# Forgetting attention and a SiLU MLP on one core: v of the first blocks on the GpSimd queue, and the first scores before the weights' transposes

## The chip, the core and the metric

The kernel runs on one core of a Trainium2 chip, in one launch. The metric is the device time of one execution in microseconds (us). A core has a matrix engine (TensorE, in the profile PE for its matmuls and PEld for its weight loads), VectorE (DVE), ScalarE (ACT), GpSimd (POOL) and SyncE (SP). They run side by side, each in the order of its own program, and wait for one another by semaphores. Sixteen DMA engines move data between the chip's memory and the core. In this kernel DMAs are issued from SyncE (the profile's queue q1), from GpSimd (q0) and, at the very end, from ScalarE.

## What is computed

The reference is an attention with a decay from forget gates f, followed by a two-layer MLP over all heads side by side:

```python
scores = scale * np.matmul(q, k.transpose(0, 1, 3, 2))
log_f = np.log(np.clip(f, 0.0001, 1.0))
cum = np.cumsum(log_f, axis=-1)
decay = cum[:, :, :, None] - cum[:, :, None, :]
causal = np.triu(np.ones((S, S), dtype=bool), k=1)
scores = np.where(causal, -1000000000.0, scores + decay)
...
x = attn_out.transpose(0, 2, 1, 3).reshape(B * S, H * D)
h = x @ w_in
g = h * (1.0 / (1.0 + np.exp(-h)))
return g @ w_out
```

There are B = 8 batches of H = 8 heads, S = 576 positions and D = 64 columns a head; w_in is 512 x 2048 and w_out 2048 x 512. All inputs and the output are float32.

## The kernel before

The decay splits into a factor of the query, which cancels in the softmax, and one of the key, so the kernel multiplies v (and a column of ones beside it, which yields the softmax's denominator) by a weight per key. The weights of all batches are made once at the start: a logarithm of f, a running sum, an exp into `wexp`, five transposes on TensorE and a copy into `w_bf` (`weights_scan()` and `weights()`).

The order on each engine is written out by hand: what the program says first on an engine runs first there.

The first 128 positions of each batch are treated apart, as "first blocks", because their queries see only their own block. For each batch b: `load_qk0(b)` brings q and k in as bf16 by two DMAs on the GpSimd queue (128 rows of 2 KB each). `load_v0(b)` brings v in as float32 by one DMA on the SyncE queue (256 KB in pieces of 64 floats) into one of four buffers `vfs[b % 4]`. `turn0(b, i)` turns q (i = 0) or k (i = 1) by matmuls with a selection matrix; ScalarE or VectorE copies the result to SBUF. `ban0` writes the causal mask into a score tile by a matmul, `scores0` adds the scores to it and takes their exp, `convert_v0(b)` multiplies v by the weights on GpSimd into `v0[b]`, `out0(b)` multiplies with v and divides, `back0(b)` transposes the result into the MLP's input. Batches 0 to 3 make the MLP's first group of 512 rows (g = 0), batches 4 and 5, and 6 and 7, groups 1 and 2 of 256 rows.

The MLP's weights come in quarters on the GpSimd queue as bf16: `load_w_in(i)` brings the columns for chunks 4i to 4i + 3 of the first product, `load_w_out(i)` the rows for part i of the second. `m1_chunk` is a chunk of the first product (TensorE into `hp`, L552; a tanh on ScalarE, L560; the product on VectorE, L561). `m2_part` is one quarter of the sum for one output tile of 128 rows (L597); parts 0 to 3 of a tile follow one another, and part i reads quarter i of w_out. `fill(us)` puts MLP matmuls for about that many microseconds at its place in the program, chosen by the writer of the order from those whose inputs are ready in program order; it does not look at the run. After groups 0 and 1 are under way, `fill(6.0, 2)` is the first with second-product parts.

Then the rest of each batch (positions 128 to 575) is done in pairs of heads: `load_qk(n)`, `load_tails(b)` and `load_v(b, c)` on SyncE's queue, `cast_qk` on GpSimd, a transposing DMA on SyncE's queue (`transposes`, L421), `scores` (L453), `attend` (L498, L507), `back` (L528). The loop over these pairs takes MLP work between its steps until the end.

`after(ap)` is a tiny DMA on SyncE's queue that reads from a tile; as it waits for the tile's load, so does all that stands behind it on SyncE's queue. Before the change there are three: behind k of batch 0 (ahead of v of batches 2 and 3), behind quarter 2 of w_in (ahead of v of batches 6 and 7), and behind quarter 1 of w_out (ahead of the loads for the main attention).

The GpSimd program before reads, in order: q,k of batches 0 to 3 among small constants; fills of the ones columns; conversion of v 0, w_in quarter 0, conversions 1 and 2, w_in 1, conversion 3, q,k of 4, w_in 2, q,k of 5, w_in 3; constants; conversion 4, w_out 0 and 1, conversion 5, w_out 2 and 3, q,k of 6 and 7; conversions 6 and 7; then the casts for the main attention.

Of the kernel before, what the change touches and what calls it, by code (L numbers as in the profile page):

```python
# [12 lines left out]
P = 128  # L13
# [5 lines left out]
def kernel(  # L19
# [10 lines left out]
    nc = tc.nc  # L30

    B, H, S, D = q.shape
    DM, DFF = moe_w_in.shape
    BH = B * H
    NCC = DM // P
# [35 lines left out]
    w_in_bf = const.tile([P, NCC, DFF], BF16, name="w_in_bf")  # L71
# [49 lines left out]
    def load_qk0(b):  # L121
        t = conv.tile([P, 2, RUN * D], BF16, name="qkb", tag="qkb")
        for i, src in enumerate((q, k)):
            nc.gpsimd.dma_start(
                out=t[:, i, :],
                in_=src[b, :, 0:P, :].rearrange("h (r c) d -> r h (c d)", c=RUN),
            )
        qk0[b] = t

    def load_v0(b):  # L130
        t = vfs[b % 4]
        nc.sync.dma_start(out=t[:, :, 0:D], in_=v[b, :, 0:P, :].rearrange("h p d -> p h d"))
        vf0[b] = t

    qst: dict[int, tuple] = {}
# [42 lines left out]
    WQ = 4  # L178

    def load_w_in(i):  # L180
        c0, c1 = i * DFF // WQ, (i + 1) * DFF // WQ
        nc.gpsimd.dma_start(out=w_in_bf[:, :, c0:c1], in_=w_in_v[:, :, c0:c1])

    def load_w_out(i):
        c0, c1 = i * NFC // WQ, (i + 1) * NFC // WQ
        nc.gpsimd.dma_start(
            out=w_out_bf[:, c0:c1, :],
            in_=moe_w_out[c0 * P : c1 * P, :].rearrange("(fc p) m -> p fc m", p=P),
        )

    def after(ap):
        nc.sync.dma_start(out=junk[0:1, 0:16], in_=ap)
# [5 lines left out]
    nc.sync.dma_start(out=f_sb[:, :], in_=f.rearrange("b h s -> (b h) s"))  # L198
    load_qk0(0)
    load_v0(0)  # L200
    load_v0(1)
    after(qk0[0][0:1, 1, 0:16])
    load_v0(2)
    load_v0(3)
    make_identity(nc, ident_bf)
    load_qk0(1)
    make_identity(nc, ident_f)
# [2 lines left out]
    load_qk0(3)  # L210
    for t in vfs:
        nc.gpsimd.memset(t[:, :, D : D + 1], 1.0)
    for i in range(2):
        for g in range(2):
            nc.vector.tensor_copy(
                out=sel[:, i, :].rearrange("p (u w r) -> p u w r", u=2, w=2)[:, g, :, :],
                in_=ident_bf[:, :].rearrange("p (r u i w) -> p u i w r", u=2, i=2, w=2)[
                    :, g, i, :, :
                ],
            )  # L220

    def keep_warm(n):
# [7 lines left out]
        out=f_sb[:, :], in0=f_sb[:, :], scalar1=1e-4, scalar2=1.0, op0=ALU.max, op1=ALU.min  # L230
# [29 lines left out]
    def weights():  # L260
        wps = pbig.tile([P, NM + 1, BH], FP32, name="wps", tag="big")
        for c in range(NM + 1):
            nc.tensor.transpose(wps[:, c, :], wexp[:, c * P : (c + 1) * P], ident_f[:, :])
        nc.vector.tensor_copy(out=w_bf[:, :, :], in_=wps[:, :, :])
# [6 lines left out]
    def turn0(b, i):  # L271
        src = qk0[b]
        if i == 0:
            qT0[b] = qktp.tile([P, NP, P], BF16, name="qkT", tag="qkT")
        dst, evac = ((qT0[b], nc.scalar.copy), (kT0[b], nc.vector.tensor_copy))[i]
        tp = pbig.tile([P, NP, NRUN, RUN], FP32, name="tp", tag="big")
        for c in range(RUN):
            for j in range(2):
                nc.tensor.matmul(  # L279
                    tp[j * D : (j + 1) * D, :, :, c].rearrange("p a r -> p (a r)"),  # L280
                    lhsT=src[:, i, c * D : (c + 1) * D],
                    rhs=sel[:, j, :],
                    start=True,
                    stop=True,
                )
        evac(
            out=dst[:, :, :].rearrange("p a t -> p (a t)"),
            in_=tp[:, :, :, :].rearrange("p a r c -> p (a r c)"),
        )

    def ban0(b):
        sc = psc.tile([P, 2, NP, P], FP32, name="sc", tag="sc")
        for i in range(2):
            nc.tensor.matmul(
                sc[:, i, :, :].rearrange("p a t -> p (a t)"),
                lhsT=ident_bf[:, :],
                rhs=ban[:, :, :].rearrange("p a t -> p (a t)"),
                start=True,
                stop=False,
            )  # L300
        return sc

    def scores0(b, sc=None):
        t = qT0.pop(b)
        fresh = sc is None
        u = upool.tile([P, 2, NP, P], BF16, name="u", tag="u")
        u0[b] = u
        if fresh:
            sc = psc.tile([P, 2, NP, P], FP32, name="sc", tag="sc")
        for p in range(NP):  # L310
            for i in range(2):
                r = slice(i * D, (i + 1) * D)
                nc.tensor.matmul(
                    sc[:, i, p, :],
                    lhsT=kT0[b][r, p, :],
                    rhs=t[r, p, :],
                    start=fresh,
                    stop=fresh or p == NP - 1,
                )
        nc.scalar.activation(  # L320
            out=u[:, :, :, :].rearrange("p i a t -> p (i a t)"),
            in_=sc[:, :, :, :].rearrange("p i a t -> p (i a t)"),
            func=ACT.Exp,
            scale=scale,
        )
# [7 lines left out]
    def convert_v0(b):  # L333
        nc.gpsimd.tensor_tensor(
            out=v0[b][:, :, :],
            in0=vf0.pop(b)[:, :, :],
            in1=w_bf[:, 0, b * H : (b + 1) * H, None].to_broadcast([P, H, D + 1]),
            op=ALU.mult,
        )
# [36 lines left out]
    def back0(b, *copies):  # L376
        xq = xqs.pop(b)[:, :, :].rearrange("p (c j) d -> p c (j d)", j=2)
        g, c0 = HEADS_OF[b]
        k = NCC // len(copies)
        for n, copy in enumerate(copies):  # L380
            tx = pbig.tile([P, k, P], BF16, name="tx", tag="big")
            for cc in range(k):
                nc.tensor.transpose(tx[:, cc, :], xq[:, n * k + cc, :], ident_bf[:, :])
            copy(out=xg(g)[:, n * k : (n + 1) * k, c0 : c0 + P], in_=tx[:, :, :])
# [239 lines left out]
    def step():  # L624

        a, c = at["m1"], at["m2"]
        can1 = a < len(M1) and M1[a][0] in ready
        g1 = M1[a][0] if a < len(M1) else NG
        g2 = M2[c][0] if c < len(M2) else NG
        if can1 and M1[a][1] == 0 and g1 > g2 + 1:  # L630
            can1 = False
        can2 = open2["w"] and c < len(M2) and g2 < g1
        if not can1 and not can2:
            return None
        if can1 and can2:
            f1 = M1[a][1] / NFC
            f2 = (c - sum(M2_OF[:g2])) / M2_OF[g2]
            want = 3 - at["last"] if abs(f1 - f2) < 0.15 else (1 if f1 < f2 else 2)
            if want == at["last"] and at["row"] >= 2 and abs(f1 - f2) < 0.25:
                want = 3 - want  # L640
            can1 = want == 1
        kind = 1 if can1 else 2
        at["row"] = at["row"] + 1 if kind == at["last"] else 1
        at["last"] = kind
        if can1:
            m1_chunk(*M1[a])
            at["m1"] += 1
            return 4 * (GW[g1] / 2.4 + 2.5)
        m2_part(*M2[c])
        at["m2"] += 1  # L650
        return 4 * (DM / 2.4 + 2.5)
# [6 lines left out]
    def fill(us_, first=0, least=0):  # L658
        if first:
            at["last"], at["row"] = 3 - first, 2  # L660
        at["left"] += us_ * 1000
        while at["left"] > 0 or least > 0:
            t = step()
            if t is None:
                at["left"] = 0.0
                return False
            at["left"] -= t
            least -= 1
        return True
# [6 lines left out]
    keep_warm(1)  # L676
    turn0(0, 1)
    bans = [ban0(0), ban0(1)]
    weights()
    setup_pool.__exit__(None, None, None)  # L680
    gpool = ctx.enter_context(tc.tile_pool(name="gpool", bufs=2))
    convert_v0(0)
    load_w_in(0)
    turn0(1, 0)
    scores0(0, bans[0])
    turn0(1, 1)
    turn0(2, 0)
    turn0(2, 1)
    scores0(1, bans[1])
    convert_v0(1)  # L690
    load_v0(4)
    out0(0, apart=True)
    scores0(2, ban0(2))
    convert_v0(2)
    load_w_in(1)
    load_v0(5)
    turn0(3, 0)
    turn0(3, 1)
    bans = ban0(3)
    out0(1, apart=True)  # L700
    scores0(3, bans)
    convert_v0(3)
    load_qk0(4)
    load_w_in(2)
    load_qk0(5)
    load_w_in(3)
    back0(0, on_act)
    out0(2)
# [11 lines left out]
    convert_v0(4)  # L720
    load_w_out(0)
    load_w_out(1)
    after(w_in_bf[0:1, NCC - 1, 3 * DFF // WQ - 16 : 3 * DFF // WQ])
    load_v0(6)
    load_v0(7)
    convert_v0(5)
    load_w_out(2)
    load_w_out(3)
    load_qk0(6)
    load_qk0(7)  # L730
    after(w_out_bf[0:1, 2 * NFC // WQ - 1, DM - 16 : DM])
    load_qk(0)
    load_tails(0)
# [42 lines left out]
    fill(6.0, 2)  # L776
    two_more(6, False)
    ready.add(2)
    fill(2.5)

# [29 lines left out]
    for m in range(NQ):  # L812
# [6 lines left out]
        if m > 0:  # L819
            back(m - 1)  # L820
            if m % 2 == 0:
                b = m // 2 - 1
# [49 lines left out]
```

## Time and profile before

| | |
|---|---|
| median of 9 runs | 351.95 us (351.21 to 352.46) |
| the profiled execution, its own time | 351.41 us |
| its span, first to last instruction | 349.6 us |
| TensorE matmuls busy | 340.9 us, 98% |
| ScalarE busy | 217.4 us, 62% |
| VectorE busy | 186.9 us, 53% |
| GpSimd busy | 123.6 us, 35% |
| moved by DMA | 47.92 MB, mean 137 GB/s |
| of it on SyncE's queue | 31.75 MB in 127184 packets |
| of it on GpSimd's queue | 15.47 MB in 9376 packets |

The profile is one execution; times in it count from its first instruction. A line of a timeline gives start, length, engine, source line, operation, and the tiles written and read; in brackets stands how long the engine was idle ahead of it, and what ended that. "Busy" of TensorE takes in matmuls that wait for nothing but their own pipeline. For a DMA the engine's line is the issue alone; its landing is told apart, as the time from issue to landing.

### The profile page before, as it was taken

The page shows a single profiled execution, that of the slowest core. Times are in us where ns is not written, and L with a number is a line of the kernel's source. Part 1 is how long each engine was busy: PE and PEld are TensorE (multiplying, and loading weights), DVE is VectorE, ACT ScalarE, POOL GpSimd, SP SyncE. Part 2 cuts the span into 40 slices and gives each one's busy share as a digit, 9 for nine tenths or more (in the row PEclk, how much of TensorE's full clock was granted, in tenths as well). Part 3 has the DMA queues.
Part 4 walks back from the last instruction along what each step waited for, and adds up shares of the span by engine and source line. Part 5 has one row for each costly group of instructions (what it writes and reads, how often), then busy time and mean ns, then how long its engine had stood idle before and what let it go on. Part 6 is the DMA issues. An engine that isn't in the chain of part 4 may idle for free.

```text
span 349.6 us, 9033 instructions
## 1 busy us (share of the span) xinstructions
PE 340.9 (98%) x3644; PEld 204.8 (59%) x3644; DVE 186.9 (53%) x411; ACT 217.4 (62%) x401; POOL 123.6 (35%) x221
## 2 busy tenths in 40 slices
PE   8989999999999999999999999999999999999994
PEld 3645565576656656566565666656656565555663
DVE  4755735355676565575555564656745553534330
ACT  5856636876587675857759567595775934544431
POOL 7894145537273163083054225326320000010001
PEclk9999999999999999999999999999999999999998
DMA  8999999999897887697487688479611000010012
GB/s 154 218 207 201 196 192 176 230 190 195 187 217 170 166 149 167 144 185 162 113 188 145 145 187 149 106 169 186 130 53 35 32 32 30 30 63 30 32 60 60
DMA packets 136761, 47.92 MB, mean 137 GB/s; under 512 B 128016, under 2 KB 134416, under 8 KB 136720
## 3 DMA queue, kind: packets, MB, share of 16 engines
q1 hardware_dynamic: 127184, 31.75, 49.1%
q0 software_dynamic: 9376, 15.47, 18.6%
q8 instruction: 28, 0.46, 0.6%
q10 hardware_dynamic: 160, 0.13, 0.1%
q14 instruction: 13, 0.11, 0.1%
HBM read 36.85 MB, written 9.44 MB: 132 GB/s over the span
## 4 chain that ended last, share of the span: by engine, by line
PE 85%; DMA 7%; ACT 3%; issue 1%; POOL 1%; DVE 1%; SPq 0%; POOLq 0%; ACTq 0%
PE po L597 35%; PE hp L552 32%; PE sc L453 7%; PE dn L498 5%; PE dn L507 3%; DMA qkb<-in_q_dram 2%; PE tx L528 2%; DMA vf<-in_v_dram 2%; DMA qkT<-qkb 1%; DMA qkb<-in_k_dram 1%; ACT u L457 1%; PE tp L279 1%; ACT osb L607 1%; DVE gt L561 1%; ACT ut L469 0%
## 5 line engine op out<-in xcount | busy, mean ns | idle before, releaser
L561 DVE SCALAR_TENSOR_TENSOR gt<-th,hp 128x384 bf16<-128x384 bf16 (+2 forms) x208 | 105.3, 522 | 81.4 <-ACT th L560 78.4
L560 ACT ACTIVATE th<-hp 128x384 bf16<-128x384 f32 (+2 forms) x208 | 95.3, 479 | 85.1 <-PE hp L552 83.4
L597 PE MATMUL po<-w_out_bf,gt 128*128 128x512 bf16 (+1 forms) x592 | 146.0, 374 | 0.0
L552 PE MATMUL hp<-x,w_in_bf 128*128 128x384 bf16 (+2 forms) x704 | 130.2, 322 | 1.1 <-DVE gt L561 0.8
L552 PEld LDWEIGHTS <-w_in_bf 128*128 128x128 bf16 x832 | 78.3, 98 | 55.6 <-issue 1.4
L457 ACT ACTIVATE u<-sc 128x1024 bf16<-128x1024 f32 (+1 forms) x96 | 74.8, 818 | 16.9 <-PE sc L453 16.8
L597 PEld LDWEIGHTS <-gt 128*128 128x128 bf16 x592 | 54.9, 98 | 48.9 <-issue 2.5
L576 POOL DMA_DIRECT2D out_dram<-osb x38 | 21.0, 553 | 167.7 <-ACT osb L607 134.7
L407 POOL TENSOR_TENSOR vp<-vf,w_bf 128x520 bf16<-128x520 f32 (+1 forms) x32 | 35.5, 1112 | 15.5 <-DMA vf<-in_v_dram 14.5
L462 DVE TENSOR_TENSOR u<-u,tri 128x768 bf16<-128x768 bf16 x32 | 21.1, 660 | 24.7 <-ACT u L457 24.7
L607 ACT ACTIVATE osb<-po 128x512 f32<-128x512 f32 (+1 forms) x37 | 22.0, 594 | 13.4 <-PE po L597 13.4
L453 PE MATMUL sc<-qkT 64*128 64x128 bf16 (+1 forms) x640 | 26.3, 207 | 0.6 <-DMA qkT<-qkb 0.5
L476 DVE TENSOR_TENSOR ut<-ut,trit 128x128 bf16<-128x128 bf16 x32 | 8.8, 276 | 28.0 <-ACT ut L469 27.9
L453 PEld LDWEIGHTS <-qkT 64*128 64x128 bf16 x640 | 18.2, 94 | 9.5 <-issue 6.1
L469 ACT ACTIVATE ut<-sc 128x640 bf16<-128x640 f32 x32 | 23.0, 719 | 0.0
L498 PEld LDWEIGHTS <-u 128*128 128x128 bf16 x576 | 20.8, 98 | 3.4 <-issue 0.4
L498 PE MATMUL dn<-vp,u 128*128 128x65 bf16 x384 | 21.8, 194 | 0.0
L516 DVE TENSOR_TENSOR xr<-dn,rec 128x448 bf16<-128x448 f32 x32 | 20.0, 624 | 1.1
L498 PE MATMUL dn<-v,u 128*128 128x65 bf16 x192 | 19.8, 194 | 0.3 <-DVE gt L561 0.3
L393 POOL CAST qkb<-qf 128x384 bf16<-128x384 f32 x32 | 16.2, 507 | 10.7 <-DMA qf<-in_q_dram 8.0
L393 POOL CAST qkb<-kf 128x384 bf16<-128x384 f32 x32 | 17.0, 531 | 7.1 <-DMA kf<-in_k_dram 7.1
L552 PE MATMUL hp<-xt,w_in_bf 128*128 128x256 bf16 x128 | 17.7, 273 | 0.0
(67 smaller groups left out, 219.3 us busy)
## 6 DMA issues: line engine op xcount, KB each, us to landing
vf<-in_v_dram SPq DMA_DIRECT2D x32, 256.0 KB, 5.0
out_dram<-osb POOLq DMA_DIRECT2D x32, 256.0 KB, 2.7
qf<-in_q_dram SPq DMA_DIRECT2D x64, 96.0 KB, 2.9
kf<-in_k_dram SPq DMA_DIRECT2D x64, 96.0 KB, 3.1
w_in_bf<-in_moe_w_in_dram POOLq DMA_DIRECT2D x4, 512.0 KB, 8.3
w_out_bf<-in_moe_w_out_dram POOLq DMA_DIRECT2D x4, 512.0 KB, 12.2
qkb<-in_q_dram POOLq DMA_DIRECT2D x8, 128.0 KB, 6.0
qkb<-in_k_dram POOLq DMA_DIRECT2D x8, 128.0 KB, 6.0
```

What stands on the lines that cost most here:

```text
L393: nc.gpsimd.tensor_copy(out=t2[:, c0 : c0 + NR, :].rearrange("p c x -> p (c x)"), in_=t[:, :, :, :].rearrange("p c h d -> p (c h d)"),)
L407: nc.gpsimd.tensor_tensor(out=vbf[b][r, c, :, :], in0=vst[b][c][r, :, :], in1=w_bf[r, c + 1, b * H : (b + 1) * H, None].to_broadcast([n, H ...
L453: nc.tensor.matmul(sc[:, i, o : o + q1 - q0], lhsT=kt, rhs=t[r, q0:q1], start=True, stop=True)
L457: nc.scalar.activation(out=u[:, :, c * SM : c * SM + w], in_=sc[:, :, 0:w], func=ACT.Exp, scale=scale)
L462: nc.vector.tensor_tensor(out=x, in0=x, in1=tri[:, None, None, :].to_broadcast([P, 2, NR, P]), op=ALU.mult,)
L469: nc.scalar.activation(out=ut[:, :, 0:3:2, :].rearrange("p k i t -> p i k t"), in_=sc[:, :, T0 : T0 + (NM + 1) * ST].rearrange("p i (k t) ...
L498: nc.tensor.matmul(dn[:, i * NR + c - 1, :], lhsT=u[:, i, o : o + P], rhs=vals(kb, i), start=(kb == 0), stop=(kb == c),)
L552: nc.tensor.matmul(hp[:, :], lhsT=w_in_bf[:, cc, fc * P : (fc + 1) * P], rhs=xg(g)[:, cc, :], start=(cc == 0), stop=(cc == NCC - 1),)
L560: nc.scalar.activation(out=th[:, :], in_=hp[:, :], func=ACT.Tanh, scale=0.5)
L561: nc.vector.scalar_tensor_tensor(out=gt[:, fc, :], in0=th[:, :], scalar=1.0, in1=hp[:, :], op0=ALU.add, op1=ALU.mult,)
L597: nc.tensor.matmul(po[:, :], lhsT=gt[:, fc, tb * P : (tb + 1) * P], rhs=w_out_bf[:, fc, m0:m1], start=(fc == 0), stop=(fc == NFC - 1),)
L607: nc.scalar.activation(out=osb[:, :], in_=po[:, :], func=ACT.Copy, scale=0.5)
```

## The change

Six v loads (batches 2 to 7) move from SyncE's queue to GpSimd's. Their places in the GpSimd program: 2 and 3 behind q,k of batch 3 and the ones columns, ahead of the first conversion; 4 and 5 each behind the q,k pair of its batch; 6 and 7 likewise. The q,k pairs of 6 and 7 move ahead of w_out quarters 2 and 3, and conversion 5 ahead of them. Two of the three `after` waits go; the one behind quarter 1 of w_out stays. Apart from that, the first scores are put ahead of the weights' transposes, and one `fill(2.5)`, the last one ahead of the main attention, becomes `fill(1.0)`.

```diff
     def load_v0(b):
         t = vfs[b % 4]
-        nc.sync.dma_start(out=t[:, :, 0:D], in_=v[b, :, 0:P, :].rearrange("h p d -> p h d"))
+        q_ = nc.sync if b < 2 else nc.gpsimd
+        q_.dma_start(out=t[:, :, 0:D], in_=v[b, :, 0:P, :].rearrange("h p d -> p h d"))
...
     load_v0(1)
-    after(qk0[0][0:1, 1, 0:16])
-    load_v0(2)
-    load_v0(3)
...
         nc.gpsimd.memset(t[:, :, D : D + 1], 1.0)
+    load_v0(2)
+    load_v0(3)
...
     bans = [ban0(0), ban0(1)]
+    scores0(0, bans[0])
     weights()
...
     turn0(1, 0)
-    scores0(0, bans[0])
     turn0(1, 1)
...
     convert_v0(1)
-    load_v0(4)
...
     load_w_in(1)
-    load_v0(5)
...
     load_qk0(4)
+    load_v0(4)
     load_w_in(2)
     load_qk0(5)
+    load_v0(5)
     load_w_in(3)
...
     load_w_out(1)
-    after(w_in_bf[0:1, NCC - 1, 3 * DFF // WQ - 16 : 3 * DFF // WQ])
+    convert_v0(5)
+    load_qk0(6)
     load_v0(6)
+    load_qk0(7)
     load_v0(7)
-    convert_v0(5)
     load_w_out(2)
     load_w_out(3)
-    load_qk0(6)
-    load_qk0(7)
     after(w_out_bf[0:1, 2 * NFC // WQ - 1, DM - 16 : DM])
...
     ready.add(2)
-    fill(2.5)
+    fill(1.0)
```

## The prediction, made before the result was known

> **What bounds the kernel now.** I read four views: busy times, TensorE's stretches, the timelines of TensorE, GpSimd and SyncE up to 66 us, and the landing time of each load of that stretch. First the page and the stretches (columns: stretch, length, busy us with instructions for PE, PEld, DVE, ACT, POOL; then clock, DMA share, GB/s):
>
> ```profile
> PE 340.9 (98%) x3644; PEld 204.8 (59%) x3644; DVE 186.9 (53%) x411; ACT 217.4 (62%) x401; POOL 123.6 (35%) x221
> 5.60:17.90 12.30, 11.64 (x223) 8.14 (x223) 8.45 (x23) 9.22 (x14) 9.61 (x19) 1.00 1.26 221
> 17.90:26.20 8.30, 7.53 (x62) 3.43 (x63) 4.95 (x8) 4.38 (x8) 8.02 (x17) 1.00 1.24 206
> 41.00:61.60 20.60, 19.95 (x195) 11.39 (x193) 8.80 (x20) 9.47 (x20) 8.26 (x11) 1.00 1.15 186
> ```
>
> TensorE is full. Its idle time is 349.6 - 340.9 = 8.7 us, of which 1.2 lie before its first matmul and 9.60 - 5.22 = 4.4 after 340 us. No edit removes TensorE work, so only the small gaps between can be won: 0.66, 0.77 and 0.65 us in these three stretches. The DMA engines move some 200 GB/s without a pause in the first 46 us, so the order of the loads decides. TensorE's timeline (start, length) shows what waits for them:
>
> ```profile
> 22.04 1.90 PE L552 MATMUL hp<-x,w_in_bf 128*128 128x512 bf16 x8 [0.51 <-DVE gt L561]
> 26.17 1.27 PE L279 MATMUL tp<-sel,qkb 128*64 128x64 bf16 x32 [0.24 <-DMA qkb<-in_q_dram]
> 41.15 2.75 PE L597 MATMUL po<-w_out_bf,gt 128*128 128x512 bf16 x12
> 43.73 0.60 PE L552 MATMUL hp<-x,w_in_bf 128*128 128x256 bf16 x4
> 44.17 1.89 PE L597 MATMUL po<-w_out_bf,gt 128*128 128x512 bf16 x8
> 61.63 0.40 PE L453 MATMUL sc<-qkT 64*128 64x128 bf16 x8 [0.52 <-DMA qkT<-qkb]
> ```
>
> The gap at 22.04 is put down to DVE, but the fifth chunk of the first MoE product is the first to read quarter 1 of w_in, and that was issued at 14.00 and took 8.0 us: 22.0. So it is a DMA wait. The 12 matmuls at 41.15 are parts 0, 1 and 2 of one output tile and read quarters 0, 1, 2 of w_out; the line at 44.17 begins with part 3 and quarter 3. GpSimd's and SyncE's timelines:
>
> ```profile
> 13.00 1.05 POOL L334 TENSOR_TENSOR v<-vf,w_bf 128x520 bf16<-128x520 f32 x1 [0.56 <-DMA vf<-in_v_dram]
> 14.00 0.81 POOL L182 DMA_DIRECT2D w_in_bf<-in_moe_w_in_dram  x1
> 23.58 1.56 POOL L186 DMA_DIRECT2D w_out_bf<-in_moe_w_out_dram  x2
> 26.15 1.54 POOL L186 DMA_DIRECT2D w_out_bf<-in_moe_w_out_dram  x2
> 29.54 0.52 POOL L124 DMA_DIRECT2D qkb<-in_k_dram  x1 [0.28 <-DMA w_in_bf<-in_moe_w_in_dram]
> 26.10 1.16 SPq L132 DMA_DIRECT2D vf<-in_v_dram  x2
> 35.79 0.50 SPq L192 DMA_DIRECT2D junk<-w_out_bf  x1
> 36.34 1.11 SPq L150 DMA_DIRECT2D qf<-in_q_dram  x2
> ```
>
> Adding each issue's time to landing gives, for GpSimd's queue: w_in 17.6, 22.0; q,k of batch 4 at 22.2 and 22.9; w_in 25.4; q,k of 5 at 26.1 and 26.7; w_in 29.2; w_out 32.4, 35.8, 39.1, 42.5; q,k of 6 at 43.4 and 44.0, of 7 at 44.8 and 46.1. They land in the order of issue. SyncE's v: batches 2 to 7 at 12.85, 13.85, 18.3, 19.3, 37.8, 44.4. So w_out quarter 2 has 42.88 - 39.1 = 3.8 us in hand, quarter 3 has 44.17 - 42.5 = 1.7.
>
> [...] The trace agrees that queues share: with SyncE quiet a w_in quarter takes 2.5 us (22.9 to 25.4, 26.7 to 29.2), beside SyncE's loads a w_out quarter takes 3.2 to 3.4. [...] no v on that queue is in this trace. [...] Here the row from 17.9 to 26.2 us, nearly all large runs, shows 206 GB/s, and the same view from 61.6 to 75 us, mostly 256 B runs, 209; I see no such loss.
>
> **The change part by part.**
>
> *Issues on GpSimd.* Six v loads come in: two before the first conversion, one behind each of the q,k pairs 4 to 7. An issue there costs 0.53 us for q or k (128 runs) and 0.80 for a weight quarter (512 runs), 0.0007 us a run; v has 1024 runs: 1.16 us. Lower bound 0.55 (a store of the same 256 KB), upper 2.3 (double). The first two then occupy GpSimd from 7.5 to 9.8. The first conversion waits for w_bf anyway; the eight score matmuls now ahead of the transposes take 0.32 us (their block starts at 9.35, the next at 9.67), so w_bf moves from 9.37 to 9.7 and the conversion from 9.52 to 9.85. Cover: out0(0) needs it at 11.47 and it ends at 10.9, so 0. At 2.3 us an issue it would end near 13.2 and cost about 1.7 us. ScalarE gets its first exp about 1 us sooner and its cast of qT0(1) 0.3 later; TensorE's order after 9.7 is as before.
>
> *v of batches 2 and 3.* Now behind q,k of 1 to 3 in one queue, with the same bytes ahead (v0, v1, f and four q,k pairs: 1.72 MB). I keep 12.9 and 14.2. Conversion 2 starts at 13.0 as now, conversion 3 (14.83) stays. The removed SyncE wait for the first k costs nobody anything, as it only held these loads. Zero, from -0.3 to +1.
>
> *v of batches 4 and 5.* They leave the stretch in which w_in quarters 0 and 1 come in. 0.52 MB at 206 GB/s is 2.5 us, so quarter 1 lands near 19.5 instead of 22.0, before its chunk at 21.5: -0.51. Batch 5's q,k have only v4 of the two ahead: 1.3 us earlier, and TensorE is there 0.5 earlier: -0.23. Sum -0.74. Their conversions run at some 25.5 and 28, well before out0(4) at 32.57.
>
> *v and q,k of 6 and 7 ahead of w_out quarters 2 and 3.* This is the large one. Quarter 1 of w_out lands at 35.8 with three quarters of v6 beside it; v6 is now behind, 0.75 x 1.27 = 0.95 less, and the unmixed v may save a little: 34.6. Then, in line: q,k 6 1.3 (25.4 to 26.7), v6 1.27, q,k 7 1.3, v7 1.27, together 5.1: 39.7. SyncE's wait for quarter 1 ends at 34.6 too, so its q, k and tail loads run beside the rest: quarters 2 and 3 at 3.2 each, as now beside SyncE: 42.9 and 46.1. Bounds for quarter 3: 43.7 (v at 1.0 us as between the landings of v2 and v3, SyncE taking nothing), 47.6 ([...]1.3 more). GpSimd's issues don't limit: they run to about 35, and the eight-in-flight limit that the 29.54 line suggests (the ninth waited for the landing of the first) asks only that w_out 1 has landed for the last issue.
> TensorE's order is fixed. It wants quarter 2 at 42.88 - 0.74 = 42.1 and waits 0.8; runs part 2 (0.86) and a chunk (0.44); is at part 3 at 44.2 and waits to 46.1: 1.9. Against 44.17 before, it is 1.9 us late. Nothing makes that up later, as it is full to the end.
>
> *Attention's start.* fill(1.0) only moves about 1.5 us of MoE matmuls behind the first scores. TensorE would be there at 61.1 + 1.9 - 1.5 = 61.5. SyncE starts its loads 1.2 us sooner, so the transposed tile lands between 60.4 and 61.6: the 0.52 wait goes.
>
> Sum: 0 + 0 - 0.74 + 2.67 (the two waits) - 0.52 = +1.4 us. The profiled execution took 351.41 us, 1.8 more than its span; +1.4 gives 352.8. The median of the nine runs is 351.95, 0.54 above it: 353.3.
>
> **Rivals.**
> 1. *w_out comes in time* (ends faster). If v in line goes at 1.0 us and SyncE's loads get little, quarters 2 and 3 land at 41.2 and 43.7 and the waits are 0 and 0.3. Then -0.74 - 0.52 + 0.3, about -1.0: 350.9. For it: [...]SyncE's first loads of this stretch took 10 us to land. Against: 1.05 MB are put ahead of two quarters that had 3.8 and 1.7 us in hand. It decides when quarter 3 lands before about 44.
> 2. *Balance.* Quarter 3 at 44.6 to 45.3, so that the wait eats the gains: 351.7 to 352.4.
> 3. *v is slow on GpSimd's queue* (twice the time, 2.6 us, or 2.3 us an issue). v3 is late by some 2 us, so conversion 3, out0(3) and the start of MoE are; quarter 3 lands 6 x 1.3 = 8 us later still. About +7: 359. Against: nothing in the trace shows that queue slower by bytes.
>
> That the change doesn't do what it says is no rival: the new order is plain in the program.
>
> **How the numbers follow.** Forecast 0.46 (own range 352.5 to 355), in time 0.34, balance 0.12, slow v 0.08. A difference under 0.2%, 0.7 us, can't be told from none. Faster 0.34, same 0.12, slower 0.54. The range is from 350.6 to 355.3; it leaves out the slow v and the ends of the bounds.
>
> **What would show it.** Right: no gap near 22 and 26; TensorE idle twice between 41 and 47, ahead of po matmuls; w_out quarters 2 and 3 landing near 43 and 46, q,k of 6 before 37; no wait at the first sc of L453. Wrong: part 3 without a wait, v issues over 1.5 us on GpSimd, or a later first hp than 17.9.

## The result, and the profile after

The changed kernel takes 354.21 us (median of 10 runs, 353.72 to 356.65) where the kernel before takes 351.95 (31 runs): a ratio of 1.0071, with a 95% interval from 1.0057 to 1.0084. It is slower by 2.3 us. The forecast was 353.3 us, in a range from 350.6 to 355.3, with slower as the likeliest side.

The profiled execution took 354.75 us, its span is 353.0. That is 3.3 us above the profiled execution of before, 1 us more than the medians differ by, so the trace shows the loss a little too large.

TensorE's stretches after (same columns as before: stretch, length, busy us with instructions for PE, PEld, DVE, ACT, POOL; clock, DMA share, GB/s):

```profile
5.60:17.90 12.30, 10.78 (x220) 7.53 (x218) 8.08 (x22) 8.91 (x13) 10.64 (x20) 1.00 1.12 201
17.90:26.20 8.30, 7.75 (x64) 3.64 (x62) 5.15 (x9) 4.86 (x9) 8.03 (x17) 1.00 1.16 207
41.00:61.60 20.60, 17.72 (x182) 10.11 (x180) 8.08 (x18) 7.59 (x17) 9.57 (x14) 1.00 1.08 199
75.00:100.00 25.00, 23.31 (x322) 15.95 (x321) 15.15 (x37) 15.91 (x34) 11.68 (x20) 1.00 0.98 185
```

Read length minus busy. From 41 to 61.6 us TensorE is idle for 2.88 us, where it was 0.65: this is the largest part of the loss. From 5.6 to 17.9 it is idle for 1.52 (before 0.66), and from 75 to 100 for 1.69 (before 25.00 - 24.42 = 0.58). From 17.9 to 26.2 it is 0.55 (before 0.77). From 100 to 340 nothing differs.

TensorE's timeline after, at the places that the prediction named:

```profile
16.57 0.42 PE L353 MATMUL dn<-v,u 128*128 128x65 bf16 x8 [0.84 <-POOL v L334]
18.50 5.34 PE L552 MATMUL hp<-x,w_in_bf 128*128 128x512 bf16 x24
26.26 0.64 PE L279 MATMUL tp<-sel,qkb 128*64 128x64 bf16 x16 [0.44 <-DMA qkb<-in_q_dram]
41.41 1.89 PE L597 MATMUL po<-w_out_bf,gt 128*128 128x512 bf16 x8
44.15 1.02 PE L597 MATMUL po<-w_out_bf,gt 128*128 128x512 bf16 x4 [0.85 <-DMA w_out_bf<-in_moe_w_out_dram]
45.01 0.60 PE L552 MATMUL hp<-x,w_in_bf 128*128 128x256 bf16 x4
47.48 1.89 PE L597 MATMUL po<-w_out_bf,gt 128*128 128x512 bf16 x8 [1.87 <-DMA w_out_bf<-in_moe_w_out_dram]
62.61 0.40 PE L453 MATMUL sc<-qkT 64*128 64x128 bf16 x8
```

The block of twelve po matmuls at 41 is now broken: two parts run, the third waits 0.85 us for quarter 2 of w_out, the fourth 1.87 us for quarter 3. The six chunks of the first product at 18.50 run through without the gap that stood at 22, and the first scores no longer wait. The new wait at 16.57 is for the conversion of v of batch 3, and behind it the first product starts at 18.50 instead of 17.92.

GpSimd and SyncE after:

```profile
15.48 1.04 POOL L334 TENSOR_TENSOR v<-vf,w_bf 128x520 bf16<-128x520 f32 x1 [0.60 <-DMA vf<-in_v_dram]
34.17 0.77 POOL L187 DMA_DIRECT2D w_out_bf<-in_moe_w_out_dram  x1 [1.30 <-DMA w_out_bf<-in_moe_w_out_dram]
36.95 0.74 POOL L187 DMA_DIRECT2D w_out_bf<-in_moe_w_out_dram  x1 [2.02 <-DMA w_out_bf<-in_moe_w_out_dram]
37.32 1.11 SPq L151 DMA_DIRECT2D qf<-in_q_dram  x2
```

Quarters 2 and 3 are issued only at 34.17 and 36.95, each just after the landing of the eighth DMA before it in GpSimd's queue (w_out quarter 0 at 33.9 and quarter 1 at 36.7), and behind everything that was put ahead of them. SyncE starts its loads for the main attention at 37.32, just behind that.

### The profile page after: what moved, and what is told of

It is laid out like the page before. It is cut to its first block, busy times and chain, and to the rows that moved or that the text cites. A ratio compares the mean times of both kernels' runs of the same rounds, so it can differ in the third digit from the quotient of the medians.

```text
span 353.0 us, 9024 instructions
## 1 busy us (share of the span) xinstructions
PE 340.2 (96%) x3644; PEld 204.3 (58%) x3644; DVE 188.1 (53%) x411; ACT 217.0 (61%) x401; POOL 128.8 (36%) x227
## 3 DMA queue, kind: packets, MB, share of 16 engines
q1 hardware_dynamic: 120880, 30.18, 45.9%
q0 software_dynamic: 9856, 17.04, 20.2%
## 4 chain that ended last, share of the span: by engine, by line
PE 80%; DMA 9%; ACT 3%; POOL 3%; issue 2%; DVE 1%; ACTq 0%; POOLq 0%
PE po L597 34%; PE hp L552 29%; PE sc L453 7%; DMA w_out_bf<-in_moe_w_out_dram 6%; PE dn L498 5%; PE dn L507 3%; DMA vf<-in_v_dram 2%; PE tx L528 2%; DMA qkb<-in_k_dram 1%; ACT u L457 1%; PE tp L279 1%; POOL qkb L124 1%; ACT ut L469 1%; ACT osb L607 1%; POOL v L334 1%
## 5 line engine op out<-in xcount | busy, mean ns | idle before, releaser
L462 DVE TENSOR_TENSOR u<-u,tri 128x768 bf16<-128x768 bf16 x32 | 22.4, 699 | 24.5 <-ACT u L457 24.5
L607 ACT ACTIVATE osb<-po 128x512 f32<-128x512 f32 (+1 forms) x37 | 22.1, 598 | 14.7 <-PE po L597 14.7
L393 POOL CAST qkb<-kf 128x384 bf16<-128x384 f32 x32 | 17.9, 560 | 1.5 <-DMA kf<-in_k_dram 1.5
```

Source lines behind the costliest of these rows:

```text
L393: nc.gpsimd.tensor_copy(out=t2[:, c0 : c0 + NR, :].rearrange("p c x -> p (c x)"), in_=t[:, :, :, :].rearrange("p c h d -> p (c h d)"),)
L462: nc.vector.tensor_tensor(out=x, in0=x, in1=tri[:, None, None, :].to_broadcast([P, 2, NR, P]), op=ALU.mult,)
L607: nc.scalar.activation(out=osb[:, :], in_=po[:, :], func=ACT.Copy, scale=0.5)
```

## The experiments

Two theories stood at first. Theory A: the two late quarters of w_out are the loss. Theory B: the late v of batch 3 at the front and the shorter fill are, and the w_out waits would be made up for. Each run below was timed against the kernel before on the same chip; `e9_sp_late` has a single execution. A diff is against the changed kernel unless it says otherwise. This table gathers the landings (issue plus time to landing, us) that the readings rest on; the last column is the transposed tile that the first scores need.

| kernel | v of 3 | w_in 1 | q of 5 | w_out 1 | w_out 2 | w_out 3 | tile |
|---|---|---|---|---|---|---|---|
| before | 13.8 | 22.0 | 26.1 | 35.8 | 39.1 | 42.5 | 61.6 |
| after | 15.3 | 20.1 | 26.3 | 36.7 | 44.1 | 47.5 | 60.4 |
| e1_wout_first | 14.6 | 19.5 | 26.8 | 35.8 | 38.3 | 40.9 | 61.5 |
| e2_before_qk_first | 13.5 | 21.7 | 26.7 | 36.4 | 43.1 | 46.8 | 60.4 |
| e8_v67_last | 14.6 | 19.5 | 25.7 | 35.3 | 40.5 | 43.9 | 61.9 |
| e9_sp_late | 14.5 | 19.4 | 26.3 | 35.3 | 42.2 | 44.7 | 64.1 |
| e6_wout_first_fill25 | 14.7 | 19.7 | 26.3 | 36.2 | 38.7 | 41.4 | 61.8 |
| e10_v45_in_line | 13.6 | 19.7 | 26.6 | 37.8 | 41.1 | 44.5 | 62.9 |
| e11_issue_early | 14.2 | 19.9 | 25.8 | 35.5 | 38.1 | 40.8 | 60.9 |
| e12_before_issue_early | 16.9 | 20.6 | 25.9 | 35.9 | 39.2 | 42.6 | 59.9 |

### The order of w_out, alone

```diff
     convert_v0(5)
+    load_w_out(2)
+    load_w_out(3)
     load_qk0(6)
     load_v0(6)
     load_qk0(7)
     load_v0(7)
-    load_w_out(2)
-    load_w_out(3)
```

> The changed kernel with w_out quarters 2 and 3 issued ahead of q,k and v of batches 6 and 7 again. Theory A (the late quarters are the loss): quarters 2 and 3 land near 39.5 and 43, both waits ahead of po (0.85 and 1.87 us) go, and part 3 starts near 44.5 instead of 47.48. The first scores then come near 60 and wait up to 0.8 us for the transposed tile, since fill(1.0) stays. Time 352.0 to 353.0 us. Theory B (the loss is v of batch 3 at the front and the shorter fill): the waits are made up for elsewhere, and the time stays within 0.7 us of 354.2.

Measured: 353.11 us, ratio 1.0046 (1.0030 to 1.0062). TensorE's timeline of this run:

```profile
41.89 2.75 PE L597 MATMUL po<-w_out_bf,gt 128*128 128x512 bf16 x12
44.92 1.89 PE L597 MATMUL po<-w_out_bf,gt 128*128 128x512 bf16 x8
61.52 0.40 PE L453 MATMUL sc<-qkT 64*128 64x128 bf16 x8 [1.42 <-DMA qkT<-qkb]
```

The twelve matmuls stand together again and both w_out waits are gone, as theory A has it. But half of what that won is spent at the first scores, which now come early (fill(1.0)) and wait 1.42 us for their tile. At the front TensorE is 0.7 us earlier in this execution and then waits 1.78 us for q of 5 instead of 0.44. The order is a cause, and it isn't the only one.

### The fill, alone

```diff
-    fill(1.0)
+    fill(2.5)
```

> The changed kernel with fill(2.5) ahead of the main attention as before. Theory A: it moves MLP work only; no wait at the first scores either way, the two w_out waits stay at 2.7 us in sum. Time 353.6 to 354.4. Theory B: the 1.1 us more of TensorE idle time from 75 to 100 us belong to the shorter fill and go. Time 353.1 or less.

Measured: 353.44 us, ratio 1.0055 (1.0035 to 1.0075), a gain of some 0.6 us on the changed kernel. The stretch from 75 to 100 us of this run:

```profile
75.00:100.00 25.00, 24.42 (x321) 16.80 (x320) 15.43 (x38) 17.80 (x36) 11.81 (x19) 1.00 1.03 186
```

TensorE is idle there for 0.58 us as in the kernel before, not 1.69. The waits in that stretch tell what of it belongs to the fill. First a line of the changed kernel, then one of this run:

```profile
93.54 1.02 PE L597 MATMUL po<-w_out_bf,gt 128*128 128x512 bf16 x4 [0.95 <-DVE gt L561]
92.19 0.60 PE L552 MATMUL hp<-x,w_in_bf 128*128 128x256 bf16 x4 [0.31 <-DVE gt L561]
```

All five traces with fill(1.0) have the first wait, at 0.94 or 0.95 us; all nine with fill(2.5) have the second in its place, at 0.31 to 0.43. This 0.6 us is the fill's. The other wait of the stretch, ahead of a dn matmul near 80 us, is 0.71 us in the changed kernel and 0.28 here, but it runs from 0.22 to 0.84 in the traces with fill(1.0) and from 0.27 to 0.99 in those with fill(2.5). Theory B is right in this point: the shorter fill isn't free. The gain in time is of the same size, but the intervals of this run and of the changed kernel overlap, so the times alone don't show it, and 353.44 lies between the two expectations.

This execution has something else in it:

```profile
16.80 0.42 PE L353 MATMUL dn<-v,u 128*128 128x65 bf16 x8 [0.86 <-POOL v L334]
17.90:26.20 8.30, 8.16 (x58) 3.71 (x60) 4.15 (x9) 4.22 (x9) 8.03 (x16) 0.79 1.11 177
```

Behind the wait for v of 3, and one of 0.54 us for the vector engine 1.2 us later, the clock that TensorE was granted is 0.79 of full speed on average; from 19 to 21 us it is 0.50. (1 - 0.79) x 8.3 / 0.5 makes 3.5 us at half speed, which costs 1.7 us of work. In this trace that is hidden, as q of 5 lands at 28.2 (26.3 in the changed kernel) and TensorE waits another 0.80 us for it. Coming to the second product at 43.23 instead of 41.41, TensorE then waits less for w_out: not at all for quarter 2 and 1.52 us for quarter 3. Three of the six executions have a mean clock of 0.993 to 0.995 and took 353.8 to 354.8 us, the three at 0.998 or 0.999 took 352.8 to 353.1.

### Both

Both edits above in one kernel.

> The changed kernel with both undone: w_out quarters 2 and 3 ahead of q,k,v of 6 and 7, and fill(2.5). In the run with the order alone the wait ahead of po had gone and one of 1.4 us had come up at the first scores; with 1.5 us more of MLP work ahead of them that wait should shrink to 0.2 or less, and TensorE's idle time from 75 to 100 us fall from 1.2 to 0.6. Theory A+ (late quarters, and a shorter fill that only pays with them late): 351.5 to 352.3 us, that is 0 to +0.5. Theory B (what remains is the front): 353 or more.

Measured: 351.14 us, ratio 0.9988 (0.9975 to 1.0002): the whole loss is gone. In ratios to the kernel before, the order alone wins 0.25%, the fill alone 0.16%, both 0.83%. The interval of both together lies clear of the changed kernel's, those of the single edits don't, so the size of each alone is uncertain. That they don't add up fits the traces, in which each alone leaves TensorE's order and the DMAs' out of step: with the quarters in time and fill(1.0) the first scores wait 1.42 us, with fill(2.5) and the quarters late a wait of 1.52 us ahead of part 3 stays. Together, the waits at both places are nil and 0.43 us.

### Half of the bytes

The kernel before, with q,k of 6 and 7 alone put ahead:

```diff
-    load_w_out(2)
-    load_w_out(3)
     load_qk0(6)
     load_qk0(7)
+    load_w_out(2)
+    load_w_out(3)
```

> The kernel before with one part of the change alone: q,k of batches 6 and 7 ahead of w_out quarters 2 and 3; v stays on SyncE's queue. Theory A: 0.52 MB are put ahead, 2.6 us. Quarter 2 lands near 41.7, in time for 42.88; quarter 3 near 45.1 against 44.17, one wait of about 0.9 us. Time 352.5 to 353.0 us, that is +0.6 to +1.1. Theory B: 351.95 as before, within 0.3.

Measured: 353.88 us, ratio 1.0076 (1.0048 to 1.0104). Quarters 2 and 3 landed at 43.1 and 46.8, 1.4 and 1.7 us later than expected, and the wait was 1.97 us. By the median, half the bytes cost as much as the whole change. But the two executions with the lowest mean clock, 0.992 and 0.995, took 355.3 and 356.4 us; the four at 0.999 or 1.000 took 352.9 to 353.9, some 1.7 above the kernel before. What the lower clock is, the profiled execution shows, the one at 0.992. TensorE's timeline and the stretch behind it:

```profile
46.89 2.74 PE L597 MATMUL po<-w_out_bf,gt 128*128 128x512 bf16 x8 [1.97 <-DMA w_out_bf<-in_moe_w_out_dram]
...
47.00:52.00 5.00, 5.00 (x28) 2.22 (x28) 0.42 (x1) 0.98 (x2) 2.50 (x6) 0.66 0.93 201
```

The first eight matmuls after the wait take 2.74 us instead of 1.89, and the clock that TensorE was granted from 47 to 52 us is 0.66 of full speed on average. From 48 to 51 us it is 0.50. At half speed that is (1 - 0.66) x 5 / 0.5 = 3.4 us, which costs 1.7 us of work on top of the wait. The wait ahead of it was 1.97 us here, and in the run with the fill alone there were two, of 0.86 and 0.54 us. In the changed kernel a wait of 1.87 us has no such stretch behind it (1.00 from 41 to 61.6 us). What decides whether the clock is halved behind a wait isn't shown.

The changed kernel, with v of 6 and 7 moved behind quarter 3 and q,k left ahead:

```diff
     load_qk0(6)
-    load_v0(6)
     load_qk0(7)
-    load_v0(7)
     load_w_out(2)
     load_w_out(3)
+    load_v0(6)
+    load_v0(7)
```

> The changed kernel with v of 6 and 7 behind w_out quarter 3, q,k of 6 and 7 still ahead of quarter 2: half of the bytes put ahead. Theory A: quarter 2 lands near 42 and isn't waited for, quarter 3 near 45.3 against 44.4, a wait of about 0.9 us in place of 2.7. Fill(1.0) stays, so the first scores may wait 0.5. Time 352.9 to 353.6 us. Theory B: 354 as the changed kernel.

Measured: 355.20 us, ratio 1.0102 (1.0076 to 1.0128). The landings were better than expected, 40.5 and 43.9, and neither quarter was waited for. Its trace shows a new wait: the first scores wait 2.00 us. The two executions with a mean clock of 0.999 and 1.000 took 353.6 (the profiled one) and 353.5 us, as theory A has it. The other four took 354.7 to 356.4, at 0.994 to 0.998, and with them the median is above that of the changed kernel. Half-clock stretches behind a wait fit the lower clock, but these executions have no trace, so this is argued and not shown.

### Whose bytes make the quarters late

```diff
-    after(w_out_bf[0:1, 2 * NFC // WQ - 1, DM - 16 : DM])
+    after(w_out_bf[0:1, NFC - 1, DM - 16 : DM])
```

> The changed kernel with SyncE's loads for the main attention held until the last w_out quarter has landed, so that nothing runs beside quarters 2 and 3. If the bytes put ahead are what makes them late: from the landing of v of 7 near 41 they take 2.5 us each, 43.7 and 46.2, and the two waits are still 0.5 and 1.2 us. If SyncE's loads beside them are: they land in time, by 43. Either way the loads come 10 us later and the first scores wait 5 us or more, so the time is 357 or more.

Measured, in one execution: 358.96 us. Quarters 2 and 3 land 2.4 and 2.5 us apart, behind v of 7 at 39.8; in the changed kernel it was 2.9 and 3.4 behind 41.2. So SyncE's loads beside them account for 1.4 us of the 2.8 by which quarter 3 is earlier. The other 1.4 had come up before w_out quarter 1 landed, where this edit changes nothing; one execution of each kernel is compared here, and they can differ by that much. The wait at both parts is gone, which the expectation had put at 0.5 and 1.2 us. The bytes put ahead alone bring the quarters to the edge; SyncE's loads beside them push them over it. The first scores then wait 4.28 us. Near the wait the clock is at 0.75 from 61.6 to 75 us, which would be (1 - 0.75) x 13.4 / 0.5 = 6.7 us if it was at half or at full speed throughout.

### The front

v of batches 2 and 3 back on SyncE's queue:

```diff
-        q_ = nc.sync if b < 2 else nc.gpsimd
+        q_ = nc.sync if b < 4 else nc.gpsimd
...
     load_v0(1)
+    after(qk0[0][0:1, 1, 0:16])
+    load_v0(2)
+    load_v0(3)
...
-    load_v0(2)
-    load_v0(3)
```

> The changed kernel with v of batches 2 and 3 on SyncE's queue behind the wait for the first k, as before. Theory A with its front term: v of batch 3 lands near 13.9 instead of 15.3, conversion 3 starts near 14.9 instead of 15.48, the 0.84 us wait ahead of dn goes and the first hp starts near 17.9 instead of 18.5. But w_out quarter 3 comes by the DMA engines' load, not by TensorE, so it lands near 47.5 again, part 3 waits longer, and the time gains 0 to 0.3 us: 353.9 to 354.2. Theory B: the 0.6 us carry to the end, 353.6 or less.

Measured: 355.89 us, ratio 1.0121 (1.0094 to 1.0148), slower than either theory has it. The profiled execution is the fastest, 354.28 us. In it the wait for v of 3 is gone, but q of 5 lands at 26.3 as ever, so TensorE, now earlier, waits 1.13 us there instead of 0.44. The 0.6 us won at the front don't get past that point. Why the other five took up to 357.7 isn't shown.

The same, with the order of w_out and fill(2.5) of before:

> As the run before in this list, with v of batches 2 and 3 back on SyncE's queue too, so that of the change only v of 4 to 7 in line and the first scores' place are left. Theory A+: the front wait of 0.4 to 0.8 us goes as well; 351.0 to 352.0 us, a little under the run without it. Theory C (SyncE's v beside GpSimd's queue spoils the weights, as the slow time of the run with these two alone put back could suggest): 353 or more.

Measured: 351.82 us, ratio 1.0012 (1.0001 to 1.0023). Theory C falls: beside the right order, v on SyncE does no harm to speak of. But it doesn't gain either: 0.24% above the kernel that differs from it only in leaving v of 2 and 3 in line, a difference at the edge of the noise. q of 5 lands at 26.8 and is waited for by 1.64 us.

### The front: v of 4 and 5, alone

The kernel before, v of 4 and 5 alone in GpSimd's queue behind their q,k pairs:

```diff
-        nc.sync.dma_start(out=t[:, :, 0:D], in_=v[b, :, 0:P, :].rearrange("h p d -> p h d"))
+        q_ = nc.gpsimd if b in (4, 5) else nc.sync
+        q_.dma_start(out=t[:, :, 0:D], in_=v[b, :, 0:P, :].rearrange("h p d -> p h d"))
...
-    load_v0(4)
...
-    load_v0(5)
...
     load_qk0(4)
+    load_v0(4)
     load_w_in(2)
     load_qk0(5)
+    load_v0(5)
```

> The kernel before with v of batches 4 and 5 alone on GpSimd's queue, each behind its q,k pair. By the prediction's own term: w_in quarter 1 lands near 19.7 and its 0.5 us wait goes, q,k of 5 come no later than before; -0.3 to -0.7 us: 351.2 to 351.6. Rival, as the changed kernel's trace suggests: GpSimd issues w_in 2 and q,k of 5 about 1 to 2 us later, q,k of 5 land at 26.3 or later while TensorE is there at 25.6, and the gain is given back: 351.7 to 352.1.

Measured: 352.94 us, ratio 1.0034 (1.0022 to 1.0047): a loss of 1.2 us, more than the rival's. w_in 1 landed at 19.7 as predicted and its wait went. But q of 5 landed at 26.6 and was waited for by 1.46 us, k by 0.36, and w_out 1 landed at 37.8, so all of SyncE's loads started later. One v less stood ahead of q of 5, and yet it was later. Stretches of one microsecond show where the time goes: first this run, then the changed kernel, then the kernel before.

```profile
15.00:16.00 1.00, 0.86 (x17) 0.52 (x15) 0.93 (x4) 1.00 (x2) 1.00 (x2) 1.00 1.32 118
16.00:17.00 1.00, 0.76 (x12) 0.45 (x12) 0.93 (x4) 0.98 (x3) 1.00 (x3) 1.00 1.01 166
```

```profile
15.00:16.00 1.00, 0.66 (x13) 0.41 (x10) 0.96 (x3) 1.00 (x2) 0.52 (x1) 1.00 0.47 70
16.00:17.00 1.00, 0.43 (x12) 0.43 (x11) 0.24 (x1) 0.71 (x2) 1.00 (x2) 1.00 0.92 131
21.00:22.00 1.00, 1.00 (x7) 0.44 (x5) 0.77 (x2) 0.61 (x2) 1.00 (x3) 1.00 0.90 140
```

```profile
15.00:16.00 1.00, 0.86 (x17) 0.52 (x15) 0.93 (x5) 1.00 (x2) 1.00 (x2) 1.00 1.21 195
16.00:17.00 1.00, 0.81 (x12) 0.51 (x12) 0.93 (x3) 0.98 (x3) 1.00 (x3) 1.00 1.24 267
21.00:22.00 1.00, 0.53 (x3) 0.04 (x1) 0.83 (x2) 0.73 (x2) 1.00 (x4) 1.00 1.25 201
```

The last two columns are the DMA engines' share and GB/s. From 15 to 17 us the rate falls to 118 and 166 GB/s in this run and to 70 and 131 in the changed kernel, where the kernel before has 195 and 267; near 21 it is 155 and 140 against 201. Over 12 to 23 us the means are 185 GB/s in this run, 179 in the changed kernel and 210 in the kernel before. In the changed kernel GpSimd had issued a quarter of w_in at 14.07 and then, as its program is in order, no load until 16.48: it waited 0.60 us for v of 3 and converted it for 1.04. In the kernel before, SyncE's v of 4 and 5, which landed at 18.3 and 19.3, were under way at that time. This became theory D: GpSimd's conversions hold its issues back and the engines run dry; it was put to the test from both sides. It doesn't serve for the dip near 21, as GpSimd issued loads without a pause from 16.5 to 22 us in the changed kernel; and in this run the engines' share stayed high from 15 to 16.

### Issue ahead of the conversions

The kernel with the order and fill of before and all v in line, with three loads each moved ahead of a conversion on GpSimd:

```diff
-    convert_v0(0)
     load_w_in(0)
+    convert_v0(0)
...
-    convert_v0(2)
     load_w_in(1)
+    convert_v0(2)
...
-    convert_v0(3)
     load_qk0(4)
+    convert_v0(3)
```

> The order with w_out first and fill(2.5), and on GpSimd three loads each ahead of the conversion that stood before them: w_in 0 ahead of conversion 0, w_in 1 ahead of conversion 2, q,k of 4 ahead of conversion 3. Theory D (with all v in GpSimd's queue the DMA engines run dry at 15 to 17 us and near 21, because GpSimd issues nothing while its conversions wait for v): the holes fill, q,k of 5 land near 25 instead of 26.3, their wait of 1.4 us falls under 0.5, w_out lands 1 us sooner; 350.0 to 350.8 us, under the kernel before. Rival (the queue isn't starved; the bytes ahead of q,k of 5 set their landing): q,k of 5 land at 26 or later and the time stays at 351.0 to 351.5.

Measured: 349.96 us, ratio 0.9957 (0.9942 to 0.9972), the fastest of all kernels here, 1.9 us under the kernel before on its chip. The same rows and TensorE's timeline:

```profile
15.00:16.00 1.00, 0.77 (x15) 0.52 (x12) 0.93 (x4) 1.00 (x2) 1.00 (x2) 1.00 1.19 177
16.00:17.00 1.00, 0.64 (x12) 0.47 (x11) 0.56 (x3) 0.85 (x3) 1.00 (x2) 1.00 1.23 202
21.00:22.00 1.00, 1.00 (x6) 0.49 (x5) 0.82 (x2) 0.73 (x2) 0.81 (x5) 1.00 1.16 189
```

```profile
25.83 1.36 PE L279 MATMUL tp<-sel,qkb 128*64 128x64 bf16 x32 [0.30 <-DMA qkb<-in_q_dram]
40.90 2.75 PE L597 MATMUL po<-w_out_bf,gt 128*128 128x512 bf16 x12
61.00 0.40 PE L453 MATMUL sc<-qkT 64*128 64x128 bf16 x8
```

These three holes are mostly filled (the mean from 12 to 23 us is 193 GB/s, still under the 210 of the kernel before), the wait for q,k of 5 is 0.30 us where the kernel with the order and the fill alone has 1.10, w_out comes in time and the first scores wait for nothing. That kernel was at 0.9988 (0.9975 to 1.0002), so the three moves together win 0.3%; which of them does isn't told apart. q of 5 landed at 25.8, not near 25 as expected, so the expectation is met in the time and the wait and only in part in the landing.

The same three moves in the kernel before, with v on SyncE's queue:

> The kernel before, v on SyncE's queue throughout, with the same three loads issued ahead of their conversions on GpSimd. Theory D (the early issue pays because all v in line leaves GpSimd's queue dry): here SyncE's v fill the holes already, the DMA engines are full from 12 to 23 us, and 1 to 2 us earlier issues change nothing: 351.5 to 352.1 us. Rival (the early issue pays by itself, whatever queue v is on): w_in quarter 1 and q,k of 5 land 1 us sooner, both waits of TensorE (0.5 and 0.2 us) go, 350.5 to 351.3 us.

Measured: 354.80 us, ratio 1.0071 (1.0044 to 1.0098). Neither side had expected a loss. Two rows of this run, TensorE's timeline and a stretch:

```profile
18.06 0.42 PE L353 MATMUL dn<-v,u 128*128 128x65 bf16 x8 [1.98 <-POOL v L334]
...
17.90:26.20 8.30, 7.37 (x36) 3.23 (x37) 3.57 (x8) 3.36 (x7) 8.03 (x17) 0.79 1.23 208
```

w_in 0 is now under way from 7.5 to 16.1 us, beside v of 2 and 3 in the other queue, and v of 3 lands at 16.9 instead of 13.8. out0(3) waits 1.98 us for it, and behind the wait the clock is at 0.79 on average for 8.3 us (0.70 from 20 to 21 us, 0.50 from 21 to 23), which is again 3.5 us at half speed. All six executions have a mean clock of 0.988 to 0.994. So the early issue won where v stands ahead of the weights in the same queue, and lost where v is in the other: that is what "in line" was good for here.

### The first scores' place

The kernel before with `scores0(0, bans[0])` ahead of `weights()`:

> The kernel before with the first scores ahead of the weights' transposes, alone. By the prediction: w_bf 0.3 us later, first exp 1 us sooner, TensorE's order the same from 9.7 us on, so nothing: 351.5 to 352.1 us. Rival (conversions and weights move by the 0.3 us, and with them quarter 1 of w_in): +0.2 to +0.4.

Measured: 351.77 us, ratio 1.0002 (0.9991 to 1.0012). Nothing, as predicted.

## Why the prediction was right, point by point

Slower was forecast, by 1.4 us with a range, and slower it is, by 2.3, for the reason that was to carry it: the two waits. Of the prediction's other signs one of being wrong came too, a first hp later than 17.9 us (18.50), and one of being right did not, as the gap near 26 us stayed.

- **w_out quarters 2 and 3.** Right, and it carries the result: the waits were predicted at 0.8 and 1.9 us and measured at 0.85 and 1.87. The run with the order alone removes both. That the sizes agree so well is luck: the landings were predicted at 42.9 and 46.1 and came at 44.1 and 47.5, and TensorE came to them 1.2 and 1.4 us later too (next points), so two errors of one size cancel. Part 3 was late by 3.3 us, not 1.9: 0.3 at its front, 2.7 of waits, and 0.3 because the matmuls of a block broken by waits took longer here (1.89 and 1.02 us for eight and four, 2.75 for twelve in one block, so 0.16 at each of two breaks).
- **w_in quarter 1.** Right: predicted near 19.5, landed at 20.1, and its wait of 0.51 us went.
- **q,k of batch 5 "1.3 us earlier".** Wrong: q landed at 26.3, where it was 26.1, and TensorE waited 0.44 and 0.17 us in place of 0.24. The step took bytes over a full rate for landing times. The rate wasn't full: it fell to 70 and 131 GB/s from 15 to 17 us, for which theory D is the account that the run with the early issues supports. With this the predicted -0.74 up to the second product became +0.26 (41.41 against 41.15). That v of 4 and 5 in line is a loss by itself is shown by its own run, 1.2 us.
- **v of batch 3 "at 14.2, zero, from -0.3 to +1".** At its edge: 15.3, and the first product starts 0.58 us later. In four other runs with the same front it landed at 14.5 to 14.7, in a fifth at 15.6. The run that undoes it gains nothing, and in its trace q of 5 is the next to be waited for.
- **v's issue "1.16 us".** 0.92 to 0.96 us; off by a fifth, with no effect.
- **v in GpSimd's queue.** The six loads came as 480 more packets there (9856 against 9376), 80 each. SyncE's queue has 6304 fewer (120880 against 127184), some 1050 a load with the two `after` loads in it, and a v has 1024 runs. V of 6 and 7 landed 1.3 and 0.8 us behind the k ahead of them, so the slow-v rival fell. The comparison of 206 with 209 GB/s doesn't show what runs of 256 B cost, as a load that casts is counted by the bf16 bytes that it writes (the trace has 512 KB for a quarter of w_in, which is 1024 KB of float32).
- **fill(1.0) "only moves about 1.5 us of MoE matmuls".** Wrong by about 0.6 us: the wait of 0.95 us at 93.54, where fill(2.5) has one of 0.31.
- **The bound of 43.7 for quarter 3.** Its own terms, 34.6 + 1.3 + 1.0 + 1.3 + 1.0 and two quarters at 2.5, make 44.2. So the rival in which w_out comes in time was put 0.5 us too fast.
- **Attention's start.** No wait, as predicted; but at 62.61 instead of 61.5, and SyncE's loads began 1 us later than before instead of 1.2 earlier, as w_out quarter 1 landed at 36.7 instead of 34.6.
- **The first scores ahead of the transposes.** Nothing, as predicted and shown.

The sum was +1.4 us and came out at +2.3 in the medians and +3.3 between the two profiled executions. The terms missing from it are the front, which lost 0.3 us where 0.7 were to be won, the 0.3 of the broken blocks, and the fill with 0.6; with them it is +3.3, as in the traces. That the medians lie only 0.9 us above the forecast is luck in part, as the profiled execution of before is 0.5 under its median and that of after 0.5 above.

What stays open: why the medians of the run with only v of 2 and 3 undone (355.89) and of the one with only v of 6 and 7 undone (355.20) are above the changed kernel's. Their profiled executions don't show it. Several of the others have a lower clock, and a half-clock stretch behind a wait is a likely part of it, not a shown one; it can't be all, as one of 356.38 us has a mean clock of 0.999. The changed kernel's own loss is not of this kind: ten of its eleven executions have 0.998 or more.

## What to carry to other kernels

Before moving a load ahead of others in a queue, find for each load that it passes the time at which its reader needs it, not the time at which it lands now: here 3.8 and 1.7 us of slack were spent on 1.05 MB, and the last wait of TensorE's fixed order set the loss. An engine that also computes may not keep its queue full (here GpSimd issued no load between 14.07 and 16.48 us, and the rate fell to 70 GB/s): put its issues ahead of what waits, or leave another queue's loads to fill the holes, but not both at once without a run, as the two together lost 2.9 us here. And a hand-set amount of filler work belongs to one arrival time; when the loads move, set it again, together with them and not alone.

## What the runs showed that was not expected

In two traces a wait of TensorE cost about twice its length. The granted clock was at half speed for an estimated 3.4 to 3.5 us, 1.7 us of work, behind a wait of 1.97 us (mean clock 0.66 from 47 to 52 us) and behind one of 1.98 (0.79 from 17.9 to 26.2). In a third trace it was so behind two waits of 0.86 and 0.54 close together (0.79 in the same stretch), hidden there by a later wait. Near one of 4.28 us the mean of 0.75 from 61.6 to 75 us makes it about twice as long. Waits of 1.87 us in the changed kernel, and of 1.78 and 2.00 us in two other runs, left it at full speed in the profiled executions, whose mean clock is 0.999 in all three. And with two weight loads 3.0 and 2.3 us further forward in their own queue (w_in 0 issued at 7.50 instead of 10.52, w_in 1 at 11.71 instead of 14.00), a load of the other queue landed 3 us later (v of 3, at 16.9 instead of 13.8), with the same bytes in all.
